# Stores and weight loads on GpSimd's queue, x of a block split three points sooner, two more units through DRAM

## The chip, the cores and the metric

The kernel runs on one core of a Trainium2 chip. The metric is the time on the device of one execution, in microseconds (us); the kernel before takes 1312.76 us, the median of three runs (1311.15 to 1312.89).

## What is computed

Three stages follow each other. A gated linear attention makes `x` (3072 tokens by 384), a mixture of four expert networks with ReLU weights its outputs by token, and a second network with `h - tanh(h)` ends it:

```python
state = alpha[t] * state + outer(k[t], v[t])         # per batch (4) and head (8), 768 steps
y[t]  = q[t] @ state                                 # 48 by 48 state; x is y with the heads side by side
h     = relu(x @ w1[e]);  out += p[:, e] * (h @ w2[e])   # e = 0..3, 384 -> 1024 -> 384
h     = out @ w_in;  g = h - tanh(h);  result = g @ w_out # 384 -> 2048 -> 384
```

All products are made to nearly full float32 precision: each operand is split into a high part (rounded) and a low part (what is left), and three matmuls of high by high, low by high and high by low are summed. So each `x` and each weight is needed twice, as a cast (ScalarE, "hi") and as a difference (VectorE or GpSimd, "lo").

## The kernel before

**Attention and expert 0.** Attention is cut into 24 units `u` of 128 tokens (six chunks by four batches). A unit goes through stages: decays (`st_c`, `st_r`, `st_prod`), scores on TensorE (`st_scores`, L302 and L307), masks on VectorE (`st_mask`), outputs on TensorE (`st_out`), copies of the outputs on ScalarE (`st_y`), a store of them to DRAM (`st_store`, tensors `xr`), a load that brings them back with channels on partitions (`st_xload`, tile `xraw`), and the split into hi (`x_hi`, L425) and lo (`x_lo`, L430). The units of the first chunk, 0 to 3, take another way: `direct` (ten matmuls on L416, the weights partly copied into zero-padded places by `place`) puts their outputs with channels on partitions at once, so that hi and lo are taken straight from PSUM and the store (`direct_y`) is only for later use.

The stages are laid out in steps called points: the table `STAGES` gives each stage an offset, and unit `u` runs a stage at point `4*(u-2)` plus the offset. `points(n)` issues all stages up to a point. The program of every engine is in the order in which the code issues it.

Beside the units runs the network of expert 0 over token blocks, four of 256 and four of 512 tokens, each in eight steps `f`: nine matmuls `mm1` (L655) on `xt` and `w`, an evacuation to `hh` and `hl` (L662, L663), and nine matmuls `mm2` (L707) behind it. Each step has two halves, and the points that the next block needs (up to `ready(u)` of its last unit) are shared out evenly over the 16 halves of a block (`share`). The last block of expert 0 has no points any more; it prepares the next stage.

**Preparation and pair stage.** Experts 1 to 3 are run in pairs of token halves and weights with sums of `x` and of weights (`pair_stage`, L740). `forms` makes the sums of `x`: ScalarE casts (L612), GpSimd takes the low parts (L613) of `ta` and `tb`, and SyncE stores them to DRAM (`xs`, `xb`, L617 and L618). `pair_load` (L628) loads them back as tiles `xt`, one third at a time. `w_pair` loads two weight tiles (`w_load`, L490, tile `wraw`), splits them (L518 on ScalarE, L521 on GpSimd) and makes the sums of weights (L525 to L528 on GpSimd). A pair stage of one expert, one pair of blocks `p` and four steps `fp` takes about 63 us; the first one begins at 318.40 us, the third pair of blocks at 452.40 us. A wide integer tensor is turned into the float32 weights of the last stage on VectorE, ScalarE and GpSimd beside it (L49 to L65, L556, L557). The last stage runs from about 860 us to the end.

**Queues.** SyncE issues all loads and all stores but those of `xr` (ScalarE). An engine runs its instructions in order, so that an issue that waits for its data holds what is behind it.

Of the kernel before, what the change touches and what calls it, by code (L numbers as in the profile page):

```python
# [183 lines left out]
def tile_kernel(ctx: ExitStack, tc: tile.TileContext, qka, a0, v, vT, pT, w12, w64, out):  # L184
# [125 lines left out]
    def st_kt(u):  # L310
        s = unit[u]
        if u < NU - B:
            s["kt"] = at.tile([P, 448], F32, name="kt", tag="kt", bufs=2)
            nc.scalar.copy(s["kt"], s["pt"])
        if 2 <= u < B:
            place(u)

    def st_mask(u):
        s = unit[u]
# [19 lines left out]
    def st_out(u):  # L339
        s = unit[u]  # L340
        update(u)
        if u < B:
            direct(u, (0, 1, 2))
            return
        s["py"] = bank(u, [112, 512], 1)
        sd = sbd[u % B]
        for j in range(4):
            t_ = slice(j * C, (j + 1) * C)
            for hf, r in halves():
                nc.tensor.matmul(s["py"][r, t_], sd[:, hf, j], s["prod"][:, t_], start=True, stop=False)  # L350
            for hf, r in halves():
                h_ = slice((2 * j + hf) * D, (2 * j + hf + 1) * D)
                nc.tensor.matmul(s["py"][r, t_], s["vt"][:, h_], s["am"][hf][:, t_], start=False, stop=True)

    def st_upd(u):
        s = unit[u]
# [16 lines left out]

    def st_y(u):
        s = unit[u]
        if u < B:
            x_hi(u, u // 2 * 256, direct_x(u))
            x_lo(u, u // 2 * 256, direct_x(u))
            direct_y(u)
            return  # L380
        s["y"] = at.tile([112, 512], F32, name="y", tag="y", bufs=2)
        for hf, r in halves():
            nc.scalar.copy(s["y"][r], s["py"][r])
# [48 lines left out]
    def direct_x(u):  # L432
        return unit[u]["py"].rearrange("p (k t) -> p k t", t=C)

    def st_xload(u):
        if u < B:
            return
        t = at.tile([P, KB, C], F32, name="xraw", tag="xraw", bufs=2)
        nc.sync.dma_start(out=t, in_=xr[u // 2][:, (u % 2) * C:(u % 2 + 1) * C].rearrange("(kb p) t -> p kb t", p=P))
        unit[u]["x"] = t  # L440

    def st_xparts(u):
        if u < B:
            return
        t0 = [t for t, n in blocks0 if t <= u * C][-1]
        x_hi(u, t0, unit[u]["x"])
        x_lo(u, t0, unit[u]["x"])
# [6 lines left out]

    def st_store(u):
        s = unit[u]
        if u < B:
            return
        for hf, r in halves():
            nc.scalar.dma_start(  # L460
                out=xr[u // 2].rearrange("(j r) t -> r j t", r=2 * D)[hf * D:(hf + 1) * D, :, (u % 2) * C:(u % 2 + 1) * C],
                in_=s["y"][r].rearrange("e (j t) -> e j t", t=C))
# [6 lines left out]
    def points(upto):  # L469
        while done[0] < upto:  # L470
            n = done[0]
            for stage, o in STAGES:
                u = (n - o) // 4 + 2
                if (n - o) % 4 == 0 and 2 <= u < NU:
                    stage(u)
            done[0] += 1

    def ready(u):
        return 4 * (u - 2) + (14 if u < B else 18)


    slot, slots, wraw = {}, {}, {}
# [1 line left out]
    def w_load(i):  # L484
        if 2 <= i < 8:

            t = acc[1 + (i - 2) // 2].rearrange("p k t -> p (k t)")[:, (i % 2) * 768:(i % 2 + 1) * 768]
        else:
            t = sp.tile([P, 768], F32, name="wraw", tag="wraw", bufs=2)
        nc.sync.dma_start(out=t, in_=w12[i])  # L490
        wraw[i] = t

    def w_hi(i):
# [105 lines left out]
    def forms(p, h, raw):  # L599
        tb = late["c"].tile([P, 2, 3, 256], F32R, name="tb", tag="tb")  # L600
        ta = late["c"].tile([P, 2, 1, 256], F32R, name="ta", tag="ta")

        x00, x10, x01, x11 = (raw[:, n, k] for n in range(2) for k in range(2))
        t1, t4, t3, t2 = x00, x10, x01, x11
        nc.vector.tensor_tensor(out=t1, in0=x01, in1=x00, op=ALU.subtract)
        nc.vector.tensor_tensor(out=t3, in0=x11, in1=x01, op=ALU.subtract)
        yield
        nc.vector.tensor_tensor(out=t2, in0=x11, in1=t1, op=ALU.subtract)
        nc.vector.tensor_tensor(out=t4, in0=x10, in1=t2, op=ALU.subtract)
        yield  # L610
        for k, (t, f) in enumerate(((ta[:, :, 0], t1), (tb[:, :, 2], t3), (tb[:, :, 0], t2), (tb[:, :, 1], t4))):
            nc.scalar.copy(t[:, 0], f)  # L612
            nc.gpsimd.tensor_tensor(out=t[:, 1], in0=f, in1=f32(t[:, 0]), op=ALU.subtract)  # L613
            if k == 1:
                yield
        c = slice(h * 256, (h + 1) * 256)
        nc.sync.dma_start(out=xs[2 * p + 1][:, :, 0:1, c], in_=f32(ta))  # L617
        nc.sync.dma_start(out=xb[p][:, :, :, c], in_=f32(tb))  # L618
        yield

    def pair_tile(k):
# [195 lines left out]
    with tc.manual_schedule():  # L817
# [110 lines left out]
        for si, st in enumerate(steps0):  # L928
            g, bi, t0, n, f, last = st
            bl = blocks0  # L930
            if f == 0:
# [9 lines left out]

                if not last:
                    first, goal = done[0], ready((bl[bi + 1][0] + bl[bi + 1][1]) // C - 1)
                    share = [first + (goal - first) * k // 16 for k in range(17)]
            ph = mm1(st)
            evac1(st, ph)
            pend.append(st)
# [183 lines left out]
```

## Time and profile before

| | us |
|---|---|
| median of three runs | 1312.76 |
| the profiled execution | 1311.73 |
| its span in the profile | 1309.8 |
| TensorE busy | 1285.7 |

In the rows, PE is TensorE (PEld its weight loads), DVE VectorE, ACT ScalarE, POOL GpSimd and SP SyncE. A row of a timeline gives the start, the duration, the engine, the line, the operation and `out<-in`; what stands in brackets is how long the engine had been idle and what ended that. Times are from the start of the span. The clock column gives the share of TensorE's full clock (2.4 GHz) that was granted; 0.50 is the lower of its two levels, 1.2 GHz.

### The profile page before, as it was taken

Reading aid. Unit: us, or ns where it says so; the run is one execution under the profiler, and the core shown is the slowest. Engines: PE = TensorE matmul, PEld = TensorE weight load, DVE = VectorE, ACT = ScalarE, POOL = GpSimd, SP = SyncE. Lnnn points to the kernel's source line nnn. Section 1 sums busy time; section 2 is a strip of 40 time slices with the busy share of each in tenths; the row PEclk is TensorE's granted clock in tenths of the full one; section 3 lists DMA queues with packets and bytes.
Section 4 is the critical chain, followed back from the end, with each engine's and each line's share of the span. In section 5 each row is a group of like instructions: output and inputs, shape, how many; then the busy total and the mean of one; then the engine's idle time right before and its main releaser. Section 6 shows DMA issues by size and latency. Waiting matters only on the chain.

```text
span 1309.8 us, 18946 instructions
## 1 busy us (share of the span) xinstructions
PE 1285.7 (98%) x6895; PEld 1054.4 (80%) x6895; DVE 899.2 (69%) x1370; ACT 616.2 (47%) x1133; POOL 544.4 (42%) x505
## 2 busy tenths in 40 slices
PE   8999999998999999999999999999999999999997
PEld 5798888786888787888888888888888888888886
DVE  8777766523457667766667766655878787878786
ACT  5334433323333333433333433335776767777765
POOL 4211211005323234622134621215787776767664
PEclk9999999999999999999999999999999999999999
DMA  8555654235472726371526251519000000000000
GB/s 274 146 147 139 174 146 143 71 120 189 166 246 78 254 70 228 101 241 58 200 77 229 89 205 65 193 53 364 34 25 1 25 1 25 1 25 1 25 2 27
DMA packets 92438, 152.47 MB, mean 116 GB/s; under 512 B 7856, under 2 KB 48304, under 8 KB 92336
## 3 DMA queue, kind: packets, MB, share of 16 engines
q1 hardware_dynamic: 82416, 146.45, 34.0%
q10 hardware_dynamic: 9920, 4.72, 1.4%
q8 instruction: 56, 0.92, 0.3%
q14 instruction: 46, 0.38, 0.1%
HBM read 114.92 MB, written 36.23 MB: 115 GB/s over the span
## 4 chain that ended last, share of the span: by engine, by line
PE 71%; DMA 1%; DVE 1%; issue 1%; ACT 1%; POOL 1%; POOLq 0%; DVEq 0%; SPq 0%; ACTq 0%
PE po L707 37%; PE ph L740 20%; PE ph L655 15%; DMA xt<-xs 1%; DMA xt<-xb 0%; DMA xb<-tb 0%; DVE hl L663 0%; DVE gg L79 0%; DVE ghu L78 0%; ACT gs L74 0%; ACT gt L72 0%; DVE gg L80 0%; ACT gs L73 0%; POOL tb L613 0%; POOL w L521 0%
## 5 line engine op out<-in xcount | busy, mean ns | idle before, releaser
L707 PE MATMUL po<-hh,w 128*128 128x512 f32 (+1 forms) x1824 | 451.5, 383 | 0.0
L707 PEld LDWEIGHTS po<-hh,w 128*128 128x128 f32 x1824 | 330.7, 189 | 72.1 <-issue 3.1
L655 PE MATMUL ph<-xt,w 128*128 128x512 f32 (+1 forms) x1440 | 326.5, 371 | 6.5 <-ACT xt L425 3.7
L655 PEld LDWEIGHTS ph<-xt,w 128*128 128x128 f32 x1440 | 252.8, 189 | 57.6 <-ACT xt L425 5.3
L707 PE MATMUL po<-hl,w 128*128 128x512 f32 (+1 forms) x912 | 248.4, 380 | 1.2 <-DVE hl L687 1.2
L740 PE MATMUL ph<-xt,w 128*128 128x512 f32 x864 | 233.6, 392 | 0.9 <-DMA xt<-xs 0.9
L707 PEld LDWEIGHTS po<-hl,w 128*128 128x128 f32 x912 | 167.5, 189 | 35.0 <-DVE hl L687 1.6
L740 PEld LDWEIGHTS ph<-xt,w 128*128 128x128 f32 x864 | 162.6, 188 | 36.8 <-DMA xt<-xs 1.3
L663 DVE SCALAR_TENSOR_TENSOR hl<-ph,hh 128x512 fp32r<-128x512 f32 (+1 forms) x136 | 85.3, 628 | 127.4 <-ACT hh L662 127.0
L662 ACT ACTIVATE hh<-ph 128x512 fp32r<-128x512 f32 (+1 forms) x136 | 74.4, 547 | 208.1 <-PE ph L655 113.0
L75 POOL TENSOR_SCALAR gmk<-gu 128x512 int32<-128x512 f32 x96 | 143.3, 1492 | 48.4 <-ACT gu L71 48.4
L687 POOL TENSOR_TENSOR hl<-gg,hh 128x512 fp32r<-128x512 f32 x94 | 121.9, 1297 | 54.0 <-ACT hh L685 54.0
L557 POOL TENSOR_TENSOR wo<-wf,wo 128x384 fp32r<-128x384 f32 x32 | 35.2, 1099 | 211.8 <-ACT wo L556 204.7
L768 ACT COPY ut<-ph 128x512 f32<-128x512 f32 x108 | 63.4, 587 | 117.2 <-PE ph L740 116.8
L733 POOL TENSOR_TENSOR acc<-acc,ptmp 128x512 f32<-128x512 f32 x51 | 65.0, 1296 | 112.8 <-DVE ptmp L729 112.8
L740 PE MATMUL ph<-xt,ws 128*128 128x512 f32 x324 | 105.4, 398 | 6.4 <-DMA xt<-xb 5.2
L71 ACT ACTIVATE gu<-ph 128x512 f32<-128x512 f32 x96 | 57.6, 600 | 113.6 <-PE ph L655 63.4
L76 DVE SCALAR_TENSOR_TENSOR ghu<-ph,gu 128x512 f32<-128x512 f32 x96 | 66.3, 691 | 53.5 <-ACT gt L72 53.1
L370 POOL TENSOR_TENSOR state<-state,fc 112x192 f32<-112x192 f32 x20 | 12.3, 614 | 161.4 <-DVE state L361 141.4
L80 DVE COPY_PREDICATED gg<-gmk,ph 128x512 f32<-128x512 int32 x96 | 71.9, 749 | 10.1 <-POOL gmk L75 0.4
L740 PEld LDWEIGHTS ph<-xt,ws 128*128 128x128 f32 x324 | 61.3, 190 | 21.3 <-issue 5.6
L79 DVE SCALAR_TENSOR_TENSOR gg<-gs,ghu 128x512 f32<-128x512 f32 x96 | 66.4, 692 | 12.7
(130 smaller groups left out, 1533.9 us busy)
## 6 DMA issues: line engine op xcount, KB each, us to landing
xt<-xs SPq DMA_DIRECT2D x54, 512.0 KB, 6.0
xt<-xb SPq DMA_DIRECT2D x27, 512.0 KB, 6.0
r<-w SPq DMA_DIRECT2D x32, 384.0 KB, 6.1
w64s<-wo SPq DMA_DIRECT2D x32, 384.0 KB, 3.0
w<-w64s SPq DMA_DIRECT2D x16, 768.0 KB, 6.1
qk<-qka SPq DMA_DIRECT2D x24, 448.0 KB, 5.1
wraw<-w SPq DMA_DIRECT2D x26, 384.0 KB, 3.6
pb<-pn SPq DMA_DIRECT2D x22, 256.0 KB, 4.4
```

What stands on the lines that cost most here:

```text
L75: nc.gpsimd.tensor_scalar(out=mk, in0=u, scalar1=T2, scalar2=None, op0=ALU.is_gt)
L76: nc.vector.scalar_tensor_tensor(out=hu, in0=ph, scalar=C4, in1=u, op0=ALU.mult, op1=ALU.mult)
L79: nc.vector.scalar_tensor_tensor(out=gg, in0=s2, scalar=B2, in1=hu, op0=ALU.add, op1=ALU.mult)
L80: nc.vector.copy_predicated(out=gg, mask=mk, data=ph)
L655: nc.tensor.matmul(ph[:, :n], w[:, a, 0, kb * P:(kb + 1) * P], x[:, b, kb, :n], start=m == 0, stop=m == len(seq) - 1)
L662: nc.scalar.activation(a[:, :n], ph[:, :n], AF.Relu)
L663: nc.vector.scalar_tensor_tensor(out=b[:, :n], in0=ph[:, :n], scalar=0.0, in1=f32(a[:, :n]), op0=ALU.max, op1=ALU.subtract)
L687: eng.tensor_tensor(out=b, in0=gg, in1=f32(a), op=ALU.subtract)
L707: nc.tensor.matmul(po[d, pool][:, :n], w[:, wi, 1, d * P:(d + 1) * P], r[:, :n], start=first and pi == 0, stop=last_ and pi == 2)
L733: nc.gpsimd.tensor_tensor(out=a_, in0=a_, in1=tmp, op=ALU.add)
L740: nc.tensor.matmul(ph, w[:, a], x[:, b], start=start and m == 0, stop=m == len(seq) - 1, skip_group_check=not start)
L768: nc.scalar.copy(t, ph)
```

## The change

Three edits. Loads of the weights from number 10 on, and the stores of the sums of `x` (`xs` and `xb` in `forms`), are issued by GpSimd instead of SyncE. Each such weight load moves 384 KB in 128 rows, each store of `ta` 256 pieces of 1 KB and each store of `tb` 768 pieces of 1 KB. The goal of a block's points (`ready`) moves from 18 to 21 for units from 4 on, and the first block runs no points in its first three halves (`idle`). Units 2 and 3 no longer take the direct way: their outputs have the usual form (eight matmuls, without a state yet), are copied, stored and loaded back as those of later units, and their stages behind the masks run four points sooner (`soon`).

```diff
--- before.py
+++ after.py
@@ -312,8 +312,6 @@
         if u < NU - B:
             s["kt"] = at.tile([P, 448], F32, name="kt", tag="kt", bufs=2)
             nc.scalar.copy(s["kt"], s["pt"])
-        if 2 <= u < B:
-            place(u)
 
     def st_mask(u):
         s = unit[u]
@@ -339,18 +337,20 @@
     def st_out(u):
         s = unit[u]
         update(u)
-        if u < B:
-            direct(u, (0, 1, 2))
-            return
         s["py"] = bank(u, [112, 512], 1)
-        sd = sbd[u % B]
-        for j in range(4):
-            t_ = slice(j * C, (j + 1) * C)
-            for hf, r in halves():
-                nc.tensor.matmul(s["py"][r, t_], sd[:, hf, j], s["prod"][:, t_], start=True, stop=False)
-            for hf, r in halves():
-                h_ = slice((2 * j + hf) * D, (2 * j + hf + 1) * D)
-                nc.tensor.matmul(s["py"][r, t_], s["vt"][:, h_], s["am"][hf][:, t_], start=False, stop=True)
+        if u >= B:
+            sd = sbd[u % B]
+            for j in range(4):
+                t_ = slice(j * C, (j + 1) * C)
+                for hf, r in halves():
+                    nc.tensor.matmul(s["py"][r, t_], sd[:, hf, j], s["prod"][:, t_], start=True, stop=False)
+                for hf, r in halves():
+                    h_ = slice((2 * j + hf) * D, (2 * j + hf + 1) * D)
+                    nc.tensor.matmul(s["py"][r, t_], s["vt"][:, h_], s["am"][hf][:, t_], start=False, stop=True)
+        else:
+            for j, hf, r, h_ in heads(u):
+                t_ = slice(j * C, (j + 1) * C)
+                nc.tensor.matmul(s["py"][r, t_], s["vt"][:, h_], s["am"][hf][:, t_], start=True, stop=True)
 
     def st_upd(u):
         s = unit[u]
@@ -373,11 +373,6 @@
 
     def st_y(u):
         s = unit[u]
-        if u < B:
-            x_hi(u, u // 2 * 256, direct_x(u))
-            x_lo(u, u // 2 * 256, direct_x(u))
-            direct_y(u)
-            return
         s["y"] = at.tile([112, 512], F32, name="y", tag="y", bufs=2)
         for hf, r in halves():
             nc.scalar.copy(s["y"][r], s["py"][r])
@@ -433,15 +428,11 @@
         return unit[u]["py"].rearrange("p (k t) -> p k t", t=C)
 
     def st_xload(u):
-        if u < B:
-            return
         t = at.tile([P, KB, C], F32, name="xraw", tag="xraw", bufs=2)
         nc.sync.dma_start(out=t, in_=xr[u // 2][:, (u % 2) * C:(u % 2 + 1) * C].rearrange("(kb p) t -> p kb t", p=P))
         unit[u]["x"] = t
 
     def st_xparts(u):
-        if u < B:
-            return
         t0 = [t for t, n in blocks0 if t <= u * C][-1]
         x_hi(u, t0, unit[u]["x"])
         x_lo(u, t0, unit[u]["x"])
@@ -454,8 +445,6 @@
 
     def st_store(u):
         s = unit[u]
-        if u < B:
-            return
         for hf, r in halves():
             nc.scalar.dma_start(
                 out=xr[u // 2].rearrange("(j r) t -> r j t", r=2 * D)[hf * D:(hf + 1) * D, :, (u % 2) * C:(u % 2 + 1) * C],
@@ -470,13 +459,15 @@
         while done[0] < upto:
             n = done[0]
             for stage, o in STAGES:
-                u = (n - o) // 4 + 2
-                if (n - o) % 4 == 0 and 2 <= u < NU:
-                    stage(u)
+
+                for u in ((n - o) // 4 + 2, (n - o) // 4 + 3):
+                    soon = o > 7 and u < B
+                    if (n - o) % 4 == 0 and 2 <= u < NU and (u == (n - o) // 4 + 2) != soon:
+                        stage(u)
             done[0] += 1
 
     def ready(u):
-        return 4 * (u - 2) + (14 if u < B else 18)
+        return 4 * (u - 2) + (14 if u < B else 21)
 
 
     slot, slots, wraw = {}, {}, {}
@@ -487,7 +478,8 @@
             t = acc[1 + (i - 2) // 2].rearrange("p k t -> p (k t)")[:, (i % 2) * 768:(i % 2 + 1) * 768]
         else:
             t = sp.tile([P, 768], F32, name="wraw", tag="wraw", bufs=2)
-        nc.sync.dma_start(out=t, in_=w12[i])
+
+        (nc.sync if i < 10 else nc.gpsimd).dma_start(out=t, in_=w12[i])
         wraw[i] = t
 
     def w_hi(i):
@@ -614,8 +606,8 @@
             if k == 1:
                 yield
         c = slice(h * 256, (h + 1) * 256)
-        nc.sync.dma_start(out=xs[2 * p + 1][:, :, 0:1, c], in_=f32(ta))
-        nc.sync.dma_start(out=xb[p][:, :, :, c], in_=f32(tb))
+        nc.gpsimd.dma_start(out=xs[2 * p + 1][:, :, 0:1, c], in_=f32(ta))
+        nc.gpsimd.dma_start(out=xb[p][:, :, :, c], in_=f32(tb))
         yield
 
     def pair_tile(k):
@@ -941,7 +933,8 @@
 
                 if not last:
                     first, goal = done[0], ready((bl[bi + 1][0] + bl[bi + 1][1]) // C - 1)
-                    share = [first + (goal - first) * k // 16 for k in range(17)]
+                    idle = 0 if bi else 3
+                    share = [first + (goal - first) * max(0, k - idle) // (16 - idle) for k in range(17)]
             ph = mm1(st)
             evac1(st, ph)
             pend.append(st)
```

The first place is GpSimd's program in the preparation (last block of expert 0). `w<-wraw` is the low part of a weight tile, `ta` and `tb` those of the sums of `x`, `sf` the sums of weights. Before:

```order
L521 TENSOR_TENSOR w<-wraw,w 128x768
L613 TENSOR_TENSOR ta<-fr,ta 128x256
L613 TENSOR_TENSOR tb<-fr,tb 128x256 x3
L521 TENSOR_TENSOR w<-wraw,w 128x768
L521 TENSOR_TENSOR ws<-sf,ws 128x384
L525 TENSOR_TENSOR sf<-wraw 128x128
L526 TENSOR_TENSOR wraw<-wraw 128x128
L527 TENSOR_TENSOR sf<-wraw 128x128
L528 TENSOR_TENSOR sf<-wraw,sf 128x128
L613 TENSOR_TENSOR ta<-fr,ta 128x256
L613 TENSOR_TENSOR tb<-fr,tb 128x256 x3
```

Now, with the first half of the sums ahead of the weights (the four rows of the sums of weights stand where the list is cut):

```order
L605 TENSOR_TENSOR ta<-fr,ta 128x256
L605 TENSOR_TENSOR tb<-fr,tb 128x256 x3
L609 DMA xs_104<-ta 256x1x256
L610 DMA xb_110<-tb 768x1x256
L513 TENSOR_TENSOR w<-wraw,w 128x768
L482 DMA wraw<-w 128x768
L513 TENSOR_TENSOR ws<-sf,ws 128x384
...
L605 TENSOR_TENSOR ta<-fr,ta 128x256
L605 TENSOR_TENSOR tb<-fr,tb 128x256 x3
L609 DMA xs_104<-ta 256x1x256
L610 DMA xb_110<-tb 768x1x256
```

Both stores of the first half of the sums, the second weight load and both stores of the second half now stand in GpSimd's own program; the low part `w<-wraw` that frees the buffer of the weight load stands behind the first two stores.

The second place is TensorE's program in the first block, around the outputs of units 2 and 3. `pa` is a bank of PSUM, `am` the masked scores, `vraw` the values, `acc_87` their padded copies. Before:

```order
L336 MATMUL pa<-vraw,kt 48x48 x8
L416 MATMUL pa<-am,acc_87 128x128
L416 MATMUL pa<-am,vraw 48x128
L416 MATMUL pa<-am,vraw 32x128
L416 MATMUL pa<-am,acc_87 128x128
L416 MATMUL pa<-am,vraw 16x128
L416 MATMUL pa<-am,vraw 48x128
L416 MATMUL pa<-am,acc_87 32x128
L416 MATMUL pa<-am,acc_87 128x128
L416 MATMUL pa<-am,vraw 32x128
L416 MATMUL pa<-am,acc_87 64x128
L655 MATMUL ph<-xt,w 128x256 x9
```

Now, around unit 3:

```order
L699 MATMUL po_475<-hl,w 128x256
L647 MATMUL ph<-xt,w 128x256 x9
L334 MATMUL pa<-vraw,kt 48x48 x8
L353 MATMUL pa<-am,vraw 48x128 x8
L699 MATMUL po_473<-hh,w 128x256
```

The ten matmuls of a unit became eight, and they stand two steps sooner: behind unit 3 come in the new order three groups of nine on L699, two on L647 and the scores of unit 4 before the first L647 of the next block, where before there was one group of nine on L707.

The third place is ScalarE's program for the same units. Before, for unit 3, `xt<-pa` is the cast of x from PSUM:

```order
L662 ACTIVATE hh<-ph 128x256
L425 CAST xt<-pa 128x3x128
L451 COPY yd<-pa 128x384
L453 DMA xr_92<-yd 128x3x128
L363 COPY state_138<-pa 48x192 x2
L662 ACTIVATE hh<-ph 128x256 x2
```

Now, for unit 3:

```order
L487 CAST w<-acc_90 128x768
L378 COPY y<-pa 48x512 x2
L363 COPY state_138<-pa 48x192 x2
L449 DMA xr_92<-y 48x4x128 x2
L420 CAST xt<-xraw 128x3x128
L654 ACTIVATE hh<-ph 128x256
L314 COPY kt<-pa 128x448
L286 ACTIVATE ab,flags<-fg 112x1024
L654 ACTIVATE hh<-ph 128x256
L420 CAST xt<-xraw 128x3x128
L654 ACTIVATE hh<-ph 128x256 x2
```

The copies and the two stores of `y` come first; the casts of x (first unit 2's, then unit 3's) read the loaded tile `xraw`, and evacuations `hh` stand behind them.

## Rows read from the trace of the kernel before

**Rows 1.** Page, engines: busy us, share of the span, instructions

```profile
PE 1285.7 (98%) x6895; PEld 1054.4 (80%) x6895; DVE 899.2 (69%) x1370; ACT 616.2 (47%) x1133; POOL 544.4 (42%) x505
```

**Rows 2.** TensorE's waits: us in total, times, longest us

```profile
PE ph L740 <- DMA xt<-xb: 5.2, 1, 5.2
PE ph L655 <- ACT xt L425: 3.7, 4, 1.4
PE ph L655 <- DVE w L499: 2.6, 2, 2.2
...
PE ph L740 <- DMA xt<-xs: 0.9, 1, 0.9
```

**Rows 3.** Timeline of PE, first block: start us, us, what [idle <-releaser]

```profile
38.28 0.49 PE L416 MATMUL pa<-am,acc 128*128 128x128 f32 x2
...
41.93 1.34 PE L655 MATMUL ph<-xt,w 128*128 128x256 f32 x9
...
55.76 1.24 PE L655 MATMUL ph<-xt,w 128*128 128x256 f32 x9
...
57.92 0.55 PE L302 MATMUL pa<-ident,prod 112*128 112x112 f32 x4
...
59.49 1.33 PE L655 MATMUL ph<-xt,w 128*128 128x256 f32 x9
...
62.44 0.42 PE L350 MATMUL pa<-prod,sbd 112*48 112x128 f32 x4
...
64.34 1.34 PE L655 MATMUL ph<-xt,w 128*128 128x256 f32 x9
```

**Rows 4.** Timeline of PE, the first block's start

```profile
21.45 2.70 PE L655 MATMUL ph<-xt,w 128*128 128x256 f32 x18 [0.57 <-ACT xt L425]
```

**Rows 5.** Issues of line 453 at 45.9 us

```profile
DMA to landing us min/median/max: 8.6/8.6/8.6
```

**Rows 6.** DMA issues: what, count, KB each, median us to landing

```profile
xr<-y ACTq DMA_DIRECT2D x40, 96.0 KB, 3.8
xraw<-xr SPq DMA_DIRECT2D x20, 192.0 KB, 2.4
...
xs<-ta SPq DMA_DIRECT2D x6, 256.0 KB, 2.4
```

**Rows 7.** Groups of ACT to 320 us, by form: busy, mean ns

```profile
L383 ACT COPY y<-pa 48x512 f32<-48x512 f32 x40 | 23.2, 579 | 26.2 <-PE pa L353 24.4 <-DMA pb<-pn 1.3
...
L425 ACT CAST xt<-xraw 128x384 fp32r<-128x384 f32 x20 | 10.3, 513 | 9.9 <-ACT y L383 6.2 <-DMA xraw<-xr 3.3 <-DMA vraw<-v 0.4
...
L363 ACT COPY state<-pa 48x192 f32<-48x192 f32 x6 | 1.9, 310 | 0.9 <-ACT yd L451 0.9
```

**Rows 8.** Timeline of POOL, 312 to 318 us

```profile
312.46 0.47 POOL L525 TENSOR_TENSOR sf<-wraw 128x128 f32<-128x128 f32 x1 [3.10 <-issue]
...
314.50 0.74 POOL L613 TENSOR_TENSOR ta<-fr,ta 128x256 fp32r<-128x256 f32 x1
...
317.29 1.84 POOL L521 TENSOR_TENSOR w<-wraw,w 128x768 fp32r<-128x768 f32 x1
```

**Rows 9.** Timeline of SyncE, issues: start us, us of the issue

```profile
308.23 0.35 SPq L490 DMA_DIRECT2D wraw<-w  x1
...
439.13 0.51 SPq L618 DMA_DIRECT2D xb<-tb  x1
```

**Rows 10.** Chain of waits, 295 to 330 us: start us, us, what

```profile
306.21 1.99 POOL w L521
...
317.36 3.94 DMA xb<-tb
...
321.36 4.32 DMA xt<-xb
```

**Rows 11.** Stretch of 2 us: busy PE, PEld, DVE, ACT, POOL; PEclk, DMA, GB/s

```profile
328.00:330.00 2.00, 2.00 (x6) 1.55 (x5) 0.00 (x0) 0.05 (x1) 0.00 (x0) 0.50 1.02 367
```

**Rows 12.** Timeline of DVE, 434 to 446 us

```profile
441.66 1.18 DVE L55 TENSOR_SCALAR t<-r 128x384 int32<-128x384 int32 x1
```

## The prediction

> **What bounds the kernel now.** I read the share of each engine first. TensorE is busy 1285.7 us of a span of 1309.8 [rows 1], the other engines at most 69% of it: what counts is TensorE's own work and the few waits between it. The list of its waits comes next [rows 2]: one of 5.2 us on the load of the sums of x, four on the cast of x in the first expert (3.7 together), two on the low parts of weights in the first block (2.6), one of 0.9 on a later load of x. The timelines of TensorE, GpSimd and SyncE at those places say what each hangs on, and the change touches all four. Nothing behind the third pair of blocks of expert 1 waits for an instruction that moves: GpSimd is busy 42% of the span [rows 1] and TensorE's list names no weight load after it, so the other loads on GpSimd's queue I cost at nothing. If that cover failed, each would cost up to one GpSimd pass of 1.84 us [rows 8].
>
> **First block.** Before, a direct unit holds TensorE from 38.28 to 41.93, 3.65 us for ten output matmuls [rows 3]. A usual unit has 16 output matmuls in 62.44 to 64.34, 1.90 us, so eight take 0.95: 2.70 less for each of two units, 5.4 of work gone. The waits on the weights should shrink as three halves now run without points: of 2.6 us I let 2 go. But unit 3's x now makes a trip through DRAM. Its output matmuls ended one group of mm2 ahead of the next block's first mm1 at 55.76; an mm1 and an mm2 together take 57.92 - 55.76 = 2.16, 1.08 each, so at 54.7. Two mm1, two mm2 and one unit's scores (59.49 - 57.92 = 1.57), 5.9 in all, now come behind them: 54.7 - 5.9 - 5.4 - 2 = 41.4. Then ScalarE makes two copies of y (0.58 each), two of the state (0.31 each) [rows 7] and two issues (0.35 each, as SyncE's cheapest in [rows 9]): the second store starts at about 43.9. Its landing: stores of this form took 3.8 in the middle, but the direct store issued at this place took 8.6 [rows 5, 6]; I take 6.2, midway. The load takes 2.4 [rows 6], the cast 0.51 [rows 7]: x is there at 53.0. TensorE has 5.9 + 1.08 = 7.0 of work to fill this and runs dry at 48.4. Block 1 starts 2.8 sooner than at 55.76, after a wait of 4.6. A wait of that length lowers the clock: after the 5.2 us of [rows 2] the clock granted was still 0.50 in 328 to 330 [rows 11]. Work resumed at 325.7 (321.36 + 4.32, [rows 10]), so some 4.3 us ran at half speed, 2.1 lost. **Term 1: -2.8 + 2.1 = -0.7.** With a landing of 3.8 x comes at 50.6, the wait is 2.2 and I charge no clock: -5.2. With 8.6 for the load as well x comes at 61.6: +5.8, and +7.9 with the clock. The issue of the load stands in SyncE's queue ahead of later units' loads, and unit 2's cast ahead of evacuations on ScalarE; both fall into the same wait.
>
> **x split three points sooner.** Of the waits on the cast, the first (0.57, [rows 4]) is in the first block and stays. The other three make 3.7 - 0.57 = 3.1 [rows 2, 4]; three points are about three of sixteen halves of a block, far more than the longest wait of 1.4. **Term 2: -3.1**; at worst 0, where the cast and the low part, now issued earlier, stand ahead of masks and make other waits of the same size.
>
> **The sums of x on GpSimd.** The chain that ends in the 5.2 us runs: low part of the second weight tile on GpSimd (306.21, 1.99), weight load (308.23), sums of weights from 312.46, `ta` (314.50), `tb`, store of `tb` (317.36, landing 3.94 later), load of it (321.36, 4.32), TensorE [rows 8 to 10]. TensorE is late only through this chain, so what lengthens it is paid in full. Before, SyncE's issues on it were 0.35 (weights) and 0.51 (`tb`); the other stores lay beside GpSimd's work. Now five issues stand in GpSimd's own order on this path: both stores of the first half ahead of the low part, the weight load behind it, both stores of the second half. The trace has no issue by GpSimd. From below, SyncE's price: 2 x (0.51 + 0.51) + 0.35 - 0.86 = +1.5. From above, GpSimd held until each store has landed: 2.4 for `ta` [rows 6], 3.94 for the first `tb`, 2.4 again, +8.7. Between them I take what GpSimd needs for a pass of as many columns as the transfer has pieces: 0.47 for 128, 0.74 for 256, 1.84 for 768 [rows 8], since a program on that engine has to make each piece: 2 x (0.74 + 1.84) + 0.47 - 0.86 = **Term 3: +4.8**. The clock is at its floor by the end of the old wait already, so a longer wait adds nothing there. x that comes earlier does not shorten this chain: it hangs on the weights.
>
> The Trainium skill, "DMA: Bandwidth & Descriptors", section "SWDGE vs HWDGE vs iDMA", says that descriptors of GpSimd's transfers are computed by its own cores, and those of SyncE and ScalarE by hardware; its section "Issuing engines are not separate DMA queues" says that another issuing engine saves only the time to start the transfer, since all share 16 engines. No run here shows either yet; both speak for a cost and against a gain of this edit.
>
> **The third pair of blocks.** Its store of `tb` on SyncE (439.13, 0.51, [rows 9]) leads over loads to the 0.9 us wait [rows 2]. Now both stores queue on GpSimd behind `tb`: 0.74 + 1.84 - 0.51 = **Term 4: +2.1**. From below, SyncE's price for the one store more, +0.5; from above, GpSimd held 2.4 by the first store and a clock loss of 2.1, +4.5. The second pair's loads have several us of room and cost nothing.
>
> **Sum.** -0.7 - 3.1 + 4.8 + 2.1 = +3.1. The profiled execution took 1311.73, so 1314.8; the median of the runs is 1312.76, 1.0 above it, and gives 1315.9. The bounds add up to -6.3 and +21.2.
>
> **Rivals.** A: GpSimd issues as cheaply as SyncE. Terms 3 and 4 fall to +1.5 and +0.5, the sum is -1.8, 1311.0. For it: moved issues leave SyncE free; against it: no row. It decides below a mean price p of 0.74 us for each of the seven issues of terms 3 and 4, where -0.7 - 3.1 - 0.86 - 0.51 + 7p is nothing. B: unit 3's trip is quick (3.8): term 1 is -5.2, sum -1.4, 1311.4. For it the usual landing, against it the 8.6 at this very place. A and B together: -6.3, 1306.5, clearly faster; this is the other side. C: GpSimd is held until its stores have landed: terms 3 and 4 are +8.7 and +2.4, sum +7.3, 1320.1. Against it: nothing in the rows shows an engine held by a landing. D: the store at 439 is held up by VectorE. Beside it VectorE runs integer passes with one input tensor, one of 1.18 us [rows 12]; if GpSimd can't write its descriptors while they run, two in the way add 2.4 to the forecast: 1318.3. The Trainium skill, "SBUF — State Buffer", section "Who interferes with whom", states this mechanism: a VectorE operation in a mode that takes both ports keeps GpSimd from writing descriptors. No run here shows it yet. E: the change moves nothing that counts, because old waits come back elsewhere (term 2 at 0, the rest as A and B): -3.2, still inside A and B.
>
> **Chances.** Forecast 0.32, A 0.18, B 0.14, A and B (with E) 0.14, C 0.14, D 0.08. Differences under 0.2%, 2.6 us, count as no change. Faster (below 1310.1): all of A and B, half of A alone and B alone less a little, 0.29. Slower (above 1315.4): somewhat over half of the forecast, C and D, 0.40. No change: 0.31. The range reaches from A and B to just beyond C, 1306 to 1321; what is left out is the long load of term 1 and the sum of several bounds.
>
> **What would show it.** Term 1: the first mm1 of block 1 starts near 53 after a wait on the cast of 4 to 5 us, with a clock at 0.50 behind it; a start before 51 is B. Term 2: the three waits on the cast of x are gone at the next blocks, and no others stand there. Term 3: the wait on the load of `tb` near 310 to 325 is 10 us instead of 5.2, and GpSimd's timeline has gaps of 0.5 to 1.8 us where the stores stand; at SyncE's price it is under 7. Term 4: the wait of 0.9 at the third pair grows to about 3. I am wrong if the wait on the load of `tb` is no longer than before, or if the first block ends later than 56.

## The result and the profile after

The changed kernel takes 1329.37 us, the median of four runs (1323.64 to 1331.75), against 1312.77 before: a ratio of 1.0123, interval 1.0086 to 1.016. That is 16.6 us slower, where 1315.9 was forecast and the range ended at 1321. The profiled execution is the shortest of the four: 1323.64 us, span 1321.4, 11.6 us over the span before. What follows accounts for those 11.6; the rest of the median is the spread, which the last experiment takes up.

First the list of TensorE's waits in the changed kernel (line, what it waited for, us in total, times, longest):

```profile
PE ph L732 <- DMA xt<-xb: 7.4, 1, 7.4
PE ph L732 <- DMA xt<-xs: 3.9, 2, 2.4
PE ph L647 <- ACT xt L420: 3.3, 2, 2.7
PE ph L647 <- DVE w L491: 2.0, 2, 1.6
PE ph L647 <- ACT w L487: 1.6, 1, 1.6
PE ph L732 <- ACT ut L760: 1.4, 1, 1.4
```

Against [rows 2], the wait on the sums grew from 5.2 to 7.4, the wait on `xs` from one of 0.9 to two of 3.9 together, and two are new: a weight cast in the first block (1.6) and ScalarE's copy `ut` (1.4). All waits of the list together are some 7 us more than before; the rest of the loss is not in it. Landmarks of TensorE's timeline show where it is (start, duration, instruction): the second step of block 1, the first pair stage, then steps of the first, second and third pair of blocks, of expert 2, and the last matmul. Before:

```profile
59.49 0.74 PE L655 MATMUL ph<-xt,w 128*128 128x256 f32 x4
...
318.40 2.20 PE L740 MATMUL ph<-xt,w 128*128 128x512 f32 x9
...
338.41 0.40 PE L740 MATMUL ph<-xt,ws 128*128 128x512 f32 x1
...
401.58 0.40 PE L740 MATMUL ph<-xt,ws 128*128 128x512 f32 x1
...
465.98 0.40 PE L740 MATMUL ph<-xt,ws 128*128 128x512 f32 x1
...
562.56 0.40 PE L740 MATMUL ph<-xt,ws 128*128 128x512 f32 x1
...
1303.33 0.40 PE L707 MATMUL po<-hl,w 128*128 128x512 f32 x1
```

After, the same places:

```profile
62.17 1.34 PE L647 MATMUL ph<-xt,w 128*128 128x256 f32 x9
...
321.10 2.20 PE L732 MATMUL ph<-xt,w 128*128 128x512 f32 x9
...
342.94 0.40 PE L732 MATMUL ph<-xt,ws 128*128 128x512 f32 x1
...
407.94 0.40 PE L732 MATMUL ph<-xt,ws 128*128 128x512 f32 x1
...
473.88 0.40 PE L732 MATMUL ph<-xt,ws 128*128 128x512 f32 x1
...
572.10 0.40 PE L732 MATMUL ph<-xt,ws 128*128 128x512 f32 x1
...
1313.33 0.40 PE L699 MATMUL po<-hl,w 128*128 128x512 f32 x1
```

The lag grows by 2.7 in the first block, by 0.0 over the rest of attention, by 1.8 at the first wait on the sums, by 1.8 at the second pair of blocks, by 1.5 at the third, by 1.6 near 560 and by 0.5 over all that follows; from the last matmul to the end it is 7.7 us instead of 6.1, another 1.6. That makes 11.6, to rounding.

The first block in the changed kernel, TensorE's timeline (in brackets the idle time before the row, and what ended it; the third row is unit 3's output matmuls, the last is the first mm1 of block 1):

```profile
25.96 0.62 PE L647 MATMUL ph<-xt,w 128*128 128x256 f32 x3 [1.63 <-ACT w L487]
26.96 1.16 PE L647 MATMUL ph<-xt,w 128*128 128x256 f32 x6 [0.38 <-DVE w L491]
...
42.67 1.05 PE L353 MATMUL pa<-am,vraw 128*48 128x128 f32 x16
...
50.80 0.98 PE L647 MATMUL ph<-xt,w 128*128 128x256 f32 x6 [1.64 <-DVE w L491]
...
55.58 2.35 PE L647 MATMUL ph<-xt,w 128*128 128x256 f32 x9 [2.72 <-ACT xt L420]
```

and the stretches of it (us, busy time of PE, PEld, DVE, ACT, POOL, then TensorE's granted clock, DMA share, GB/s):

```profile
25.00:30.00 5.00, 3.66 (x23) 3.19 (x25) 4.27 (x8) 3.46 (x7) 3.33 (x8) 0.76 0.73 255
30.00:35.00 5.00, 5.00 (x38) 4.63 (x36) 3.63 (x6) 1.30 (x3) 0.39 (x1) 0.56 0.49 158
...
55.00:60.00 5.00, 4.42 (x20) 4.42 (x21) 3.35 (x6) 0.90 (x2) 0.20 (x1) 0.50 0.52 138
```

In the kernel before, TensorE's clock was at 1.00 in all of these stretches; the last of them there:

```profile
55.00:60.00 5.00, 5.00 (x50) 4.74 (x49) 2.18 (x3) 1.66 (x5) 2.21 (x4) 1.00 0.77 212
```

Unit 3's output matmuls take 0.98 (42.67 to 43.65) instead of 3.65, as forecast, and block 1 starts at 55.58, 0.2 sooner than in [rows 3]. But the clock fell twice: to 0.56 in 30 to 35, behind waits of 1.63 and 0.38, and to 0.50 in 55 to 60, behind waits of 1.64 and 2.72. The second cost 2.9 us between 55.58 and 62.17 alone: the same mm1, mm2 and scores took 6.59 instead of 3.73.

The waits on weights did not shrink either: 3.6 in all (1.6 on the cast, 2.0 on the low part) instead of 2.6.

GpSimd's timeline in the preparation gives the price of its issues, which the trace before did not have:

```profile
308.91 0.70 POOL L609 DMA_DIRECT2D xs<-ta  x1
309.53 0.94 POOL L610 DMA_DIRECT2D xb<-tb  x1
310.25 2.10 POOL L513 TENSOR_TENSOR w<-wraw,w 128x768 fp32r<-128x768 f32 x1
312.64 0.58 POOL L482 DMA_DIRECT2D wraw<-w  x1 [0.30 <-POOL w L513]
...
321.43 0.64 POOL L609 DMA_DIRECT2D xs<-ta  x1
322.03 0.88 POOL L610 DMA_DIRECT2D xb<-tb  x1
```

About 0.6 for a weight load of 128 pieces, 0.7 for 256 pieces and 0.9 for 768: it hardly grows with the pieces. For the same transfers SyncE's issues have medians of 0.35 to 0.54 in the kernel before; two of them are in [rows 9].

### The profile page after: what moved, and what is told of

Its sections match the earlier page's. It is cut to its first block, busy times and chain, and to the rows that moved or that the text cites. A ratio compares the mean times of both kernels' runs of the same rounds, so it can differ in the third digit from the quotient of the medians.

```text
span 1321.4 us, 18914 instructions
## 1 busy us (share of the span) xinstructions
PE 1288.4 (97%) x6887; PEld 1058.6 (80%) x6887; DVE 899.0 (68%) x1370; ACT 613.1 (46%) x1125; POOL 565.4 (43%) x539
## 4 chain that ended last, share of the span: by engine, by line
PE 87%; DMA 4%; DVE 2%; ACT 2%; issue 1%; POOL 1%; SPq 0%; ACTq 0%; DVEq 0%; POOLq 0%
PE po L699 41%; PE ph L647 21%; PE ph L732 20%; PE pa L307 2%; PE pa L346 2%; PE pa L349 1%; DMA wraw<-w 1%; DMA xt<-xs 1%; ACT y L378 1%; PE pa L334 1%; DMA xr<-y 1%; DMA vraw<-v 1%; POOL w L513 0%; POOL tb L605 0%; DMA xb<-tb 0%
## 5 line engine op out<-in xcount | busy, mean ns | idle before, releaser
L699 PE MATMUL po<-hh,w 128*128 128x512 f32 (+1 forms) x1824 | 449.4, 382 | 0.0
L699 PEld LDWEIGHTS po<-hh,w 128*128 128x128 f32 x1824 | 333.6, 190 | 69.3 <-ACT acc L712 1.3
L647 PE MATMUL ph<-xt,w 128*128 128x512 f32 (+1 forms) x1440 | 331.4, 375 | 6.9 <-ACT xt L420 3.3
L647 PEld LDWEIGHTS ph<-xt,w 128*128 128x128 f32 x1440 | 253.2, 190 | 60.9 <-ACT xt L420 3.7
L699 PE MATMUL po<-hl,w 128*128 128x512 f32 (+1 forms) x912 | 248.8, 381 | 1.2 <-DVE hl L679 1.2
L699 PEld LDWEIGHTS po<-hl,w 128*128 128x128 f32 x912 | 167.9, 189 | 34.8 <-DVE hl L679 1.6
L80 DVE COPY_PREDICATED gg<-gmk,ph 128x512 f32<-128x512 int32 x96 | 71.9, 749 | 10.1 <-POOL gmk L75 0.4
```

Of the source, the lines that this page charges most:

```text
L80: nc.vector.copy_predicated(out=gg, mask=mk, data=ph)
L647: nc.tensor.matmul(ph[:, :n], w[:, a, 0, kb * P:(kb + 1) * P], x[:, b, kb, :n], start=m == 0, stop=m == len(seq) - 1)
L699: nc.tensor.matmul(po[d, pool][:, :n], w[:, wi, 1, d * P:(d + 1) * P], r[:, :n], start=first and pi == 0, stop=last_ and pi == 2)
```

## Experiments

Each kernel was timed beside the kernel before on the same chip; the ratio is to that. "Before" in an edit is the kernel before. The first four split the change into its parts.

**The queue edit alone.**

```diff
-        nc.sync.dma_start(out=t, in_=w12[i])
+        (nc.sync if i < 10 else nc.gpsimd).dma_start(out=t, in_=w12[i])
...
-        nc.sync.dma_start(out=xs[2 * p + 1][:, :, 0:1, c], in_=f32(ta))
-        nc.sync.dma_start(out=xb[p][:, :, :, c], in_=f32(tb))
+        nc.gpsimd.dma_start(out=xs[2 * p + 1][:, :, 0:1, c], in_=f32(ta))
+        nc.gpsimd.dma_start(out=xb[p][:, :, :, c], in_=f32(tb))
```

> Before with the queue edit alone (weight loads from number 10 on and stores of the sums of x by GpSimd). Theory P (prices add up as the trace of the change shows them): the first wait on the sums grows by 1.8 us, the second and third pair of blocks wait 1.8 and 1.5 more, one more wait of 1.4 near 560, and 1.6 more from the last matmul to the end: +8, about 1320 to 1321, with a spread as small as before's (2 us). Theory V (the 8 us between runs of the changed kernel come from the GpSimd queue): the same sum or more, and runs that differ by 5 us or more. Theory C (they come from TensorE's clock in the first block): spread below 3 us here.

1325.15 us (1323.49 to 1326.56), ratio 1.011, interval 1.0095 to 1.0126: 13.5 us of the 16.6. Its four runs spread by 3 us, those of the changed kernel by 8. That suggests that the 8 us need the other edits too; four runs each do not show it, and the weight loads alone (below) spread by 6 us in ten runs. In its profile TensorE waits at the second and third pair of blocks, where before it waited 0 and 0.91:

```profile
393.50 1.43 PE L740 MATMUL ph<-xt,w 128*128 128x512 f32 x5 [2.11 <-DMA xt<-xs]
...
460.65 2.50 PE L740 MATMUL ph<-xt,w 128*128 128x512 f32 x5 [3.42 <-DMA xt<-xs]
```

**The points alone** (`ready` 21 and `idle`).

> Before with the points alone (split three points sooner, no points in the first three halves of block 0). Theory P: the three waits on the cast of x (3.1 us) go, but small waits come in their place, 0 to -3 us, 1310 to 1313. Theory C: with no points in the first halves TensorE waits 1.6 us at about 26 us for a weight cast, its clock falls to 0.50 there as in the changed kernel, and some of 3 us is lost: 1312 to 1315, and a spread above 3 us.

1310.13 us (1308.59 to 1312.61), ratio 0.9991, interval 0.9982 to 1.0: 1.5 us faster at the middle, at the edge of the noise, as the interval reaches 1.0. In its profile TensorE waits 1.62 at 25.75 for the weight cast as in the changed kernel, but there the clock stayed at 1.00 in 25 to 35. The same wait is once followed by a dip and once not. The queue edit moves nothing that runs before 300 us, so it is hardly what makes the difference.

**Units 2 and 3 through DRAM alone.**

> Before with the third edit alone (units 2 and 3 through DRAM, stages behind the masks sooner). Theory P: 5.4 us of matmuls less, against a wait for x of unit 3 and the clock it costs; block 1 starts within 2 us of 55.8 and the sum is 0 to +3, 1312 to 1316. Theory C: a dip of the clock to 0.50 after that wait in all runs, a spread above 3 us as the wait is now longer and now shorter.

1313.31 us (1312.15 to 1315.77), ratio 1.0011, interval 1.0002 to 1.002: 1.7 us slower. In its profiled execution, the longest of its eleven runs (1315.77), block 1 starts at 58.02 after a wait of 5.03 on the cast of x, with the clock at 0.50 in 55 to 60. The 5.4 us of matmuls that are gone do not pay for that wait.

**Both without the queue edit.**

> The changed kernel with the queue edit undone. Theory P: +2.7 at the end of the attention's first block, nothing more behind: 1314 to 1316. Theory C: the spread of the changed kernel (8 us) stays, 1314 to 1323. Theory V: the spread is gone (below 3 us) and the time is near 1315.

1314.10 us (1312.38 to 1315.84), ratio 1.0018, interval 1.0009 to 1.0027: 2.5 us slower. 13.5 and 2.5 add up to 16.0, against 16.6 for the whole change and 14.7 in its second set of runs (the last experiment): within the spread, the queue edit and the other two simply add up. The other two do not: alone they are -1.5 and +1.7, which makes +0.2, and together +2.5. Why is not shown; in the profiles the longest wait on weights is 2.13 with the third edit alone and 3.77 with both. In the profile of both, the longest of its eleven runs, the clock stays at 1.00 behind the wait at 25.75, and unit 3's output matmuls start at 39.41 instead of 42.67: the first dip costs the changed kernel some 3 us up to there. The dip of this kernel comes later, with 0.50 in 50 to 60. Its eleven runs spread by 3.5 us, so the 8 us do not come from these two edits alone.

The next three take the queue edit apart.

**Weight loads alone on GpSimd's queue** (the first line of the diff above).

> Before with only the weight loads from number 10 on issued by GpSimd. Theory I (the cost is the issue on the path): one load on the path to the first wait on the sums at 0.6 to 0.8 us instead of 0.35, less than +1 there; the wait of 1.3 near 560 appears; nothing at the second and third pair of blocks; with 2 us more from the last matmul to the end, +3 to +4. Rival X (the cost is the sharing of the transfer engines between two queues): the loads delay others wherever they fall, +5 or more.

1316.93 us (1313.9 to 1320.06), ratio 1.0035, interval 1.0023 to 1.0047: 4.3 us, between theory I's +4 and X's +5, so the total decides nothing. There is no wait longer than before at the second and third pair; the first wait on the sums is 7.15, and the wait on `ut` of 1.23 near 556 is this edit's. The two us more from the last matmul to the end, which are in theory I's sum, did not come. The first wait is 2 us longer, where theory I had less than 1: the weight load on that path landed in 5.9 us instead of 4.1. With the whole queue edit the same load landed in 3.4; why it took 5.9 here is open.

**Stores alone on GpSimd's queue** (the other two lines).

> Before with only the stores of the sums of x issued by GpSimd. Theory I (issues of 0.7 and 0.9 us in GpSimd's order): +1.5 at the first wait, +1.1 at the third pair of blocks, +2 at the end: +4 to +5. Rival X (the store, no longer ahead of SyncE's loads of xs in one queue, shares the transfer engines with them): its landing at the second and third pair takes 7 us instead of 4.6, waits of 2 and 3.4 us stand there, +8 to +10.

1322.47 us (1321.3 to 1324.21), ratio 1.0071, interval 1.0054 to 1.0088: 9.8 us, as rival X said. The waits on `xs` are 2.36 and 3.81 at the second and third pair. 4.3 and 9.8 make 14.1, about the 13.5 of the two together.

**The same stores on ScalarE's queue** (`nc.scalar` in their place).

> Before with the stores of the sums of x issued by ScalarE, a second queue whose issues are as cheap as SyncE's. Rival X (sharing with SyncE's loads): the landing of the store of tb at the second and third pair of blocks is 7 us as with GpSimd's queue, and the waits there stay. Theory S (a store issued by GpSimd is slow in itself): the landing is 4 to 5 us as with SyncE. ScalarE is held where the store waits for GpSimd, so the total may rise for that alone: 1312 to 1325, and only the landings decide.

1318.69 us (1318.14 to 1320.3), ratio 1.0049, interval 1.0032 to 1.0066. ScalarE is held by the stores, as TensorE's waits of 1.91 and 4.11 before 321 show (on `hl`, which VectorE makes from ScalarE's `hh`), so the total tells little. The landing of the store of `tb` for the second pair decides. In the order: with SyncE before (issued at 375.0), with GpSimd (379.1 in the kernel with the stores alone), with ScalarE (376.8):

```profile
DMA to landing us min/median/max: 4.6/4.6/4.6
```

```profile
DMA to landing us min/median/max: 8.2/8.2/8.2
```

```profile
DMA to landing us min/median/max: 6.9/6.9/6.9
```

A queue whose issue costs ScalarE 0.52 us, as SyncE's does SyncE, is nearly as slow to land: the slow landing is not GpSimd's. What the two have in common stands in SyncE's timeline. Before, it issued the store first and the loads of `xs` behind it:

```profile
375.00 0.52 SPq L618 DMA_DIRECT2D xb<-tb  x1
375.61 2.02 SPq L628 DMA_DIRECT2D xt<-xs  x2
379.67 1.84 SPq L628 DMA_DIRECT2D xt<-xb  x3
```

In the changed kernel SyncE issues the two loads of 512 KB as soon as their buffers are free, at 378.83, and the store follows at 380.04 from GpSimd:

```profile
378.83 1.65 SPq L620 DMA_DIRECT2D xt<-xs  x2
387.47 1.83 SPq L620 DMA_DIRECT2D xt<-xb  x3
389.39 3.56 SPq L620 DMA_DIRECT2D xt<-xs  x4
```

Ahead of the load of `xb` SyncE waits 6.9 us for the store to land instead of 2.0, and the loads behind move with it.

**Stores on GpSimd's queue, those two loads behind the loads of `tb`.**

```diff
-        used((0, 0))
...
-        used((0, 1))
...
-        used((1, 1), (0, 2))
+        used((1, 1), (0, 0), (0, 1), (0, 2))
```

> Stores of the sums of x on GpSimd's queue as in the earlier run of that edit, but SyncE's two loads of xs that were issued just before the store of tb are issued behind the loads of tb. Rival X (the store shares the engines with those loads): the store of tb lands in 4.4 to 4.9 us at the second and third pair of blocks instead of 7 to 8, and the waits on xs there change with the order of the loads; the total may move either way by 3 us from 1322, as the first third of x is then loaded late. Theory S (slow in itself): the landing stays at 7 to 8.

1324.65 us (1322.64 to 1324.95), ratio 1.01, interval 1.0085 to 1.0115. The store of `tb` for the second pair now lands in

```profile
DMA to landing us min/median/max: 4.4/4.4/4.4
```

and for the third in 4.4 as well: of the landing, rival X is confirmed. The store was issued at 376.4, at the same time as in the profile of the whole queue edit (376.6), where it took 7.0. The total is no better, since the first third of x is now loaded last and TensorE waits for it in three pieces (0.67, 0.42 and 0.80 at the second pair; 0.30, 0.42 and 0.79 again at expert 2, where the edit holds too). So no run gives the landing back without a new wait, and how much of the 9.8 us is the landing's is not shown by a time.

**The split three points sooner, alone** (`ready` 21 without `idle`).

> Before with the split three points sooner and nothing else (points in the first halves as before). If the gain of the edit on the points is in the later blocks: the three waits on the cast of x (3.1 us) go, 1309 to 1311. If it came from the first halves without points: no gain here, 1311 to 1313.

1312.21 us (1311.47 to 1314.13), ratio 0.9999, interval 0.9989 to 1.0008: no gain. The three waits on the cast are gone from TensorE's list, as forecast. The list of its weight loads (PEld), 50 to 318 us, shows what came in their place. First the row of the kernel before, then that of this one:

```profile
PEld pa L307 <- ACT y L383: 0.3, 1, 0.3
```

```profile
PEld pa L307 <- ACT y L383: 2.5, 8, 0.5
```

Scores wait eight times, 2.5 us in all, for ScalarE's copy of y, which frees their bank of PSUM. So what the edit on the points gains, it gains by the empty halves of block 0: in the profile of the points alone the scores of block 1 start at 55.91 instead of 57.92.

**Without the queue edit, weight loads 8 and 9 two steps later.**

```diff
-                if bi == 0 and f == 5:
+                if bi == 0 and f == 7:
                     w_load(8)
```

> The changed kernel without its queue edit, and the two weight loads 8 and 9 (384 KB each) issued two steps later in block 0, behind the load of unit 3's x. Theory L (x of units 2 and 3 is late because its stores and loads share the transfer engines with these loads): the stores land in 3 to 5 us instead of 8.6, the loads in 2.5 to 4 instead of 6 to 7, the waits of 3.8 and 4.0 us in block 0 shrink to under 2 together and the clock stays up: 1308 to 1311. Rival (the loads of later units alone fill the engines): waits and clock as before, 1313 to 1315.

1312.62 us (1311.18 to 1313.84), ratio 1.0008, interval 0.9998 to 1.0017: 1.2 us over before instead of 2.5. The profiles are of unlike runs, the shortest of its ten here and the longest of eleven without this edit, so what they show is the landings more than the time. Unit 3's load takes 2.4 us instead of 6.2, and the wait on its cast is 1.30 instead of 3.98; but its first store still lands in 8.7 (8.6), and the wait of 3.9 on the weights at 49.75 stays with its dip of the clock. Theory L holds for the load and fails for the store. What delays the store then is open; the loads of the next unit, issued at 41.80 and 42.62, are next to it.

**The points alone, and the wait on the sums filled.** To weigh the clock by itself, matmuls of zeros run in the wait that the kernel before had already.

```diff
+        if (g, p, fp) == (1, 0, 0):
+            pw = late["p"].tile([P, 512], F32, name="ph", tag="po0")
+            for n in range(22):
+                nc.tensor.matmul(pw, late["wu"][:, 0:P], late["wu"], start=n == 0, stop=n == 21)
         product(pa, [(s2, t2)], False, False)
```

> Before with the edit on the points alone, and 22 matmuls of zeros on TensorE that fill the wait on the sums of x at about 316 to 323 us (their result is not used). If the wait costs more than its length because the clock falls to 0.50 behind it, 2 us come back: 1307.5 to 1308.5, with the clock at 1.00 in 320 to 332. If not, 1310 as without them, or 1311 where the zeros outlast the wait.

1308.56 us (1306.9 to 1311.51), ratio 0.9979, interval 0.9971 to 0.9988: faster than before by 2.9 us, and faster than both kernels. The rows of TensorE's timeline and of the stretch that was at 0.50 in [rows 11]:

```profile
318.28 4.70 PE L784 MATMUL ph<-wu 128*128 128x512 bf16 x21
323.84 0.93 PE L740 MATMUL ph<-xt,ws 128*128 128x512 f32 x3 [0.86 <-DMA xt<-xb]
```

```profile
328.00:330.00 2.00, 2.00 (x11) 1.62 (x10) 0.69 (x1) 0.35 (x2) 0.57 (x2) 1.00 1.05 398
```

The wait is as long (318.28 to 323.84), and the three matmuls behind it take 0.93 instead of 1.62. The points alone gave 1.5 beside another set of runs, so about 1.4 us is the clock's, somewhat under the 2.1 that the prediction read from the rows.

**The changed kernel again.**

> The changed kernel once more, for a second profile. If the edits add up: 13.5 (queue edit alone) and 2.5 (the other two) over before, about 1327.5. If the spread of its runs (8 us in the first four) is made of waits behind which the clock falls or stays: a profile that is some us longer than the first one shows lower granted clock or longer waits in the stretches 20 to 65, 320 to 335, 390 to 400 and 455 to 470, and is the same as the first elsewhere.

1326.84 us (1325.88 to 1329.88), ratio 1.0121, interval 1.0103 to 1.0139. Its profiled execution (1326.12) is 2.5 us longer than the first. At the third pair of blocks TensorE waits 3.25 instead of 2.41, and behind that the clock falls, which it did not in the first profile (1.00 in both stretches):

```profile
463.46 2.50 PE L732 MATMUL ph<-xt,w 128*128 128x512 f32 x5 [3.25 <-DMA xt<-xs]
```

```profile
460.00:465.00 5.00, 1.75 (x5) 1.25 (x5) 2.23 (x3) 1.20 (x3) 1.10 (x1) 0.84 1.01 353
465.00:470.00 5.00, 5.00 (x20) 4.03 (x19) 2.64 (x5) 1.19 (x3) 0.49 (x1) 0.82 0.92 355
```

The landmark at 473.88 is then at 476.57, 2.7 later, while the dip of the first block was milder (0.72 in 55 to 60). So the spread is made, at least in part, of dips that follow a wait in one execution and not in another. For the two runs at 1331.6 and 1331.8 there is no profile, but their mean granted clock is on record: 0.989 and 0.987, against 0.991 in the profiled 1323.64. As an estimate from these, the 0.004 between them, of 1329 us, is up to 5 us of the 8 between the longest run and the shortest. Which waits the dips stand behind there is not shown.

## Why the prediction was wrong

- **The sign of the sum was right, its size was not:** +3.1 forecast, +16.6 measured. The rivals C and D, the dearest that had a chance, gave 1320.1 and 1318.3. Both halves missed by as much: terms 3 and 4 price the queue edit at +6.9, and it cost 13.5; terms 1 and 2 price the other two at -3.8, and they cost 2.5. The price of GpSimd's issue, on which most of the chances hung, was not what decided: the seven issues of terms 3 and 4 took 0.76 in the mean, and with that the prediction's own sum is +0.2.
- **Term 3 (+4.8)** was too dear. The pass by pieces (0.47, 0.74, 1.84) was the wrong measure: issues take 0.58, 0.70 and 0.94. By the prediction's formula that is 2 x 1.64 + 0.58 - 0.86 = +3.0; the landmark behind the first wait lags by 1.8 more. With the queue edit alone the wait ended 1.8 later and the landmark 1.1.
- **Term 4 (+2.1), and the second pair "costs nothing".** This is the step of the queue edit that failed most. The issues were moved past SyncE's loads, and the prediction counted their own time but left the landing as it was (4.6). In the profile of the queue edit alone the landmarks stand at 339.51, 405.12 and 473.67, so that the lag grows by 1.1 up to the first pair of blocks, by 2.4 at the second and by 4.1 at the third; TensorE waits there 2.11 and 3.42 instead of 0 and 0.91, the latter with the clock at half behind it. The two profiles of the changed kernel have 1.8 and 1.5, and 2.7 and 4.3. The landings of 7 to 8 us on two other queues and of 4.4 behind reordered loads show that what was lost is the place ahead of the loads. The several us of room at the second pair were eaten by 3 of landing on top of the issues and of the lag before. That the wait at the third pair came out near the "about 3" of the prediction (2.41, 3.25 and 3.42) is luck: the issues gave 1.1 of it by the prediction's formula, where 2.1 were forecast, and the landing the rest.
- **"The other loads on GpSimd's queue I cost at nothing"** failed near 560: the two loads of a pair stand behind three passes of GpSimd (the last ends at 555.6), ScalarE's cast waits for the first of them, and `ut` stands behind the cast. It cost 1.4 to 1.6, inside the 1.84 that the prediction named for a cover that fails. The weight loads alone cost 4.3 us; in their profile 2.0 more stand in the first wait, behind the landing of 5.9.
- **Term 1 (-0.7)** came out as +2.7 in the first profile. Its matmuls were gone as forecast. Block 1 started at 55.6, 2.6 later than 53.0 and inside the bounds of the trip: the second store was issued at 45.0 instead of 43.9, and landed in 7.4 instead of 6.2. Behind the late issue stands a dip of the clock that the term left out (behind the wait of 1.6 at 25.96, worth some 3 us), and waits on weights of 2.0 before unit 3's outputs, where the sum left 0.6. The trip itself was too short in the sum: from the second store to block 1 it allowed 9.1, and the profiles with units 2 and 3 through DRAM have 10.1 (late weight loads), 10.6 (the changed kernel), 12.7 (the third edit alone) and 15.5 (both edits without the queue edit). The other 0.8 is the second dip, 2.9 instead of the 2.1 charged, though the wait ahead of it was 2.7 and not 4.6. The bound of -5.2 charged no clock for a wait of 2.2; dips stand behind waits of 1.6 and 2.7 here, so the wait of 5.2, from which the price was taken, is not the shortest that has one. In the medians the third edit alone costs 1.7.
- **Term 2 (-3.1)** was at its bound of 0 (the split alone, 1312.21 against 1312.64). The waits went as forecast and 2.5 of them came back as waits for PSUM, in pieces of 0.3 that TensorE's own list leaves out. The prediction had named masks, not the copies.
- **Rivals C and D** did not happen: GpSimd went on with its next pass 0.7 us after the issue of each store of `tb` before the first wait, which landed after 4.3 to 4.7, and beside VectorE's passes at the third pair its issues took 0.68 and 0.93 with the queue edit alone, as elsewhere. The Trainium skill's lock of VectorE against descriptors ("SBUF — State Buffer", section "Who interferes with whom") shows in none of these rows.
- **Not foreseen:** 1.6 us more from the last matmul to the end. It is there in the three profiles with the whole queue edit (7.7 to 8.2 instead of 6.1) and not with either half (6.2 and 6.4); its cause is open.
- **The Trainium skill,** "DMA: Bandwidth & Descriptors", section "Issuing engines are not separate DMA queues", was the rule that bore: transfers from all queues interleave on the same engines. The landings of 6.9 on ScalarE's queue and 8.2 on GpSimd's, against 4.6 and 4.4 when no load was ahead, agree. The prediction read it as no gain and did not draw that a store can lose its place.

## What to carry to other kernels

When a transfer moves to another queue, write down what it stood ahead of as well as what it stood behind: here the order of one queue protected the store (4.6 us), and on another queue it shared the engines with the loads in flight (6.9 to 8.2). Its landing has to be priced beside its issue. Read waits removed on TensorE together with the list of its weight loads, where the time can come back in pieces too short for the first list. And price a new wait with the clock that may fall behind it, or fill it with work.

## What the runs showed of the hardware

- An issue by GpSimd takes it 0.54 to 0.94 us here, for 128 to 768 pieces of 1 to 3 KB (medians 0.55 for 128, 0.68 for 256, 0.93 for 768); SyncE's, for the same transfers, have medians of 0.35 to 0.54.
- A store of 768 KB lands in 3.9 to 4.8 us with no load just ahead of it, on any of the three queues, and in 6.9 to 8.2 where another queue had issued two loads of 512 KB in the 0.7 to 2.2 us before.
- The granted clock falls to 0.50 behind waits of 1.6 to 2.7 us in some executions and not in others: behind the wait of 1.62 at 25.8 it fell in both profiles of the changed kernel and stayed at 1.00 in four others with the same wait (the points alone, with and without the filled wait, and both edits without the queue edit, with and without the late loads). Behind the wait of 2.41 at the third pair it stayed at 1.00 in the first profile. In two profiles (weight loads alone, stores alone) block 0, which those edits leave as before, ran 1.6 us longer for such a dip in 30 to 40.
